# Moving routing work into the prologue of a fused attention and expert kernel, and reordering its first loads

## The chip, the cores and the metric

The kernel runs on one core of one Trainium2 chip. The metric is the device time of one execution in microseconds, the median of three runs. A core has five engines that run their own instruction streams: TensorE (PE, with its weight loads shown apart as PEld), VectorE (DVE), ScalarE (ACT), GpSimd (POOL) and SyncE (SP). They wait for one another through semaphores. SyncE, ScalarE and GpSimd also issue DMA transfers, which sixteen DMA engines carry out.

## The reference

Two stages, one after the other. The first is attention with a relative position bias over 8 batches of 8 heads, 576 positions and head size 64. The second sends each of the 4608 rows of its output to one of 8 experts, chosen by a hash of the token's id, and applies a two-layer network.

```python
scores = scale * np.matmul(q, k.transpose(0, 1, 3, 2))
scores = scores + bias_table[bucket].transpose(2, 0, 1)[None]   # bucket: by |i - j|
attn = softmax(scores)
x = np.matmul(attn, v)            # then (B*S, H*D) = (4608, 512)

expert_idx = token_ids * np.int64(2654435761) % np.int64(E)     # E = 8
for e in range(E):
    mask = expert_idx == e
    h = np.maximum(x[mask] @ w1[e], 0.0)                        # 512 -> 1024
    out[mask] = h @ w2[e]                                       # 1024 -> 512
```

The multiplier leaves 1 modulo 8, so the expert is the lowest three bits of the id, which the kernel takes with a bitwise and.

## The kernel before

**Attention.** The work is cut into 32 pairs of heads (8 batches of 4 pairs), run in order by `for n in range(NP + 1)`. For each pair q and k are loaded as float32 (`load`, buffers qf and kf, four deep), cast to float16 by VectorE (`cast_q`, `cast_k`), transposed on TensorE through a PSUM tile with the tag "aux" (two buffers) and copied to SBUF by VectorE (`transpose_q` gives qt, `transpose_k` gives kz). kz holds two heads with zeros between them; `z_init` writes the zeros once for each of its three buffers. `scores(n, g)` for g = 0 to 3 multiplies kz by qt into a PSUM tile with the tag "ps" (two buffers of three banks), and ScalarE takes the exponential into att. The bias comes in as a factor: `band` multiplies parts of att by ebd on VectorE, a table of exponentials of the bias differences; `low_bands` does the rest of a pair one pair later. For the last key tile there is a compact copy, ebs, made by `make_ebs` with two transfers; before it is there `band` takes two half-height products from ebd. `av_steps(n - 1)` runs one pair behind: it multiplies att by vt and vs (values with a column of ones), then VectorE takes the reciprocal of the sums (rcp) and writes the normalised rows to x_all. v is cast by ScalarE (`cast_v`), the last 64 rows of each batch's v (vsf to vs) by GpSimd (`cast_vs`).

**Order.** All five engines follow an order written out by hand (`manual_schedule`): each engine executes its instructions in the order in which the Python code emits them. So a line's place in the code is its place in the queue of its engine.

**The bias table.** In the prologue the 32-bucket table (tbl) is multiplied by a constant one-hot matrix (ohsb) on TensorE, ScalarE takes the exponential (ebsb), and a transfer writes it to memory (F_d, shown as t_f). `load_bias` then reads it back with a shifted window for each row into ebd: pair 0 from the queues of ScalarE and SyncE, pair 1 and pairs 2 and 3 from GpSimd's.

**Routing.** `route()` is a generator; each `yield` ends a step, and the loops advance it. Its steps are: te (lowest bits of the ids in raw, two instructions of VectorE); tef (cast to float16); tps, ef (transposed to tokens on partitions by TensorE, mask added by VectorE) and the memsets of keep on GpSimd; oh (one-hot by expert); rps, inc, rnk (two matmuls into a tile with the tag "ps", a scan over it and a subtraction on VectorE); then mx, mxl with flag, a product, rank, ovf, sel and ds2, one step each. ds2 is the slot of each token in its expert's list. From n = 14 GpSimd writes the 40 lists of tokens to memory (`name_slot`, shown as t_id), three for a pair, paced by copies that wait for rcp.

**The first expert's rows.** At n = 28 SyncE reads the lists back (xid) and at n = 29 stores x of batch 6; at n = 30 GpSimd gathers five tiles of 128 rows for expert 0 (`gather(0, B - 1)`, xg). Rows of the last batch are not in memory then, so they come from x_all by a one-hot product: `hot_slots()` is a generator whose first step is an iota on GpSimd (ramp) and a copy of the slots (slot), and whose five further steps each compare ramp with one column (hot). It is advanced at g = 0, 1 and 3 of n = 30 and n = 31. `first_rows` transposes gathered tiles (xr, xt) within n = 31; `first_slots` does the one-hot product (xin).

**Experts.** For each of the 8 experts: hps (first layer), h, ops (second layer), and an indirect store of the rows by GpSimd.

Of the kernel before, what the change touches and what calls it, by code (L numbers as in the profile page):

```python
# [13 lines left out]
I32 = mybir.dt.int32  # L14
# [17 lines left out]
def kernel(  # L32
# [11 lines left out]
    nc = tc.nc  # L44
# [8 lines left out]
    P = 128  # L53
# [139 lines left out]
    with tc.tile_pool(name="at", bufs=1) as at, tc.tile_pool(  # L193
# [50 lines left out]
            if what == "qkv":  # L244
                load_v(n)

        def load_v(n):
            b, m = pairs[n]
            for hh in range(2):
                nc.sync.dma_start(  # L250
                    out=vf[n % 4][:, hh, :, :],
                    in_=v[b, 2 * m + hh, :NB4].rearrange(
                        "(t p) d -> p t d", p=P
                    ),
                )
# [16 lines left out]
        def cast_q(n):  # L272
            qh[n] = at.tile([PB, 2 * NBLK, 2, D], F16, name="qh", bufs=3)
            nc.vector.tensor_copy(  # L274
                out=qh[n][:, :, :, :].transpose([0, 2, 1, 3]),
                in_=qf[n % 4][:, :, :, :].rearrange(
                    "p h k (c d) -> p h (k c) d", c=2
                ),
            )
# [238 lines left out]
        def band(n, g, lo=0):  # L518
            m = pairs[n][1]
            att = atts[n]  # L520
            if g < NDUO:
                w0 = D * g - (HALF - P)
                hi = UA if lo == 0 else HALF
                a0, a1 = max(-w0, lo), min(WB - w0, hi)
                if a0 >= a1:
                    return
                part = (att[:, 2 * g : 2 * g + 2, :QW] if lo == 0 else
                        att[:, 2 * g : 2 * g + 2, QW:])
                a = part.rearrange("p c (o u) -> p c o u", o=2)[
                    :, :, :, a0 - lo : a1 - lo  # L530
                ]
                nc.vector.tensor_tensor(  # L532
                    out=a, in0=a,
                    in1=ebd[:, :, m, :, a0 + w0 : a1 + w0].transpose(
                        [0, 2, 1, 3]
                    ),
                    op=ALU.mult,
                )
            else:
                a = att[:, NU - 1, :QW].rearrange("p (o u) -> p o u", o=2)[  # L540
                    :, :, :EW
                ]
                if n < NPAIR:
                    for hh in range(2):
                        w0 = EW - HD * hh
                        r = slice(D * hh, D * hh + D)
                        nc.vector.tensor_tensor(
                            out=a[r], in0=a[r],
                            in1=ebd[r, :, m, hh, w0 : w0 + EW], op=ALU.mult,
                        )  # L550
                else:
                    nc.vector.tensor_tensor(
                        out=a, in0=a, in1=ebs[:, :, m, :], op=ALU.mult
                    )
# [102 lines left out]
        )  # L657
        ohsb = at.tile([2 * NB, FW], F16, name="ohsb")
        nc.scalar.dma_start(out=ohsb[:, :], in_=OH_d.ap())
        nc.gpsimd.dma_start(out=ident[:, :], in_=I128_d.ap())  # L660
        load(0, "qk")
        load(1, "qk")

        def z_init(i):
            nc.vector.memset(kz[i][D:P, :S].bitcast(I32), 0)
            nc.vector.memset(kz[i][:D, S:].bitcast(I32), 0)

        idle = at.tile([P, 512], F16, name="idle")
        nc.vector.memset(idle[:, :].bitcast(I32), 0)
# [36 lines left out]
                )  # L706

        z_init(1)
        z_init(2)
        FH = FW // 2  # L710
        for i in range(2):
            nc.tensor.matmul(
# [9 lines left out]
        nc.scalar.dma_start(  # L722
            out=F_d.ap(), in_=ebsb[:, :, :].rearrange("h a b -> h (a b)")
        )
        def load_bias(eng, m0, m1, b2):
            for o in range(2):
                eng.dma_start(
                    out=ebd[b2::2, o, m0:m1, :, :].rearrange(
                        "p m h w -> p (m h) w"
                    ),  # L730
                    in_=bass.AP(
                        F_d.ap().tensor,
                        2 * m0 * FW + (o - b2 + 1) * FY + 1,
                        [[1, D], [FW, 2 * (m1 - m0)], [1, WB]],
                    ),
                )

        def make_ebs():
            for hh in range(2):
# [6 lines left out]
                    ),  # L746
                )

        cast_q(0)
        cast_k(0)  # L750
        v_init(0)
        vs_init(0)
        for i in range(1, 4):
            v_init(i)
        nobody = at.tile([P, NSLOT // P, 2], I32, name="nobody")
        nc.gpsimd.memset(nobody[:, :, :], BIG)
        load_bias(nc.scalar, 0, 1, 0)
        load_bias(nc.sync, 0, 1, 1)
        load(0, "v")
        load(2, "qk")  # L760
        load_vs(0, nc.gpsimd)
        ids = moe_token_ids.bitcast(I32).rearrange(
            "(b s c) -> b s c", b=B, c=2
        )
        nc.gpsimd.dma_start(out=raw[:1, :, :], in_=ids[B - 1 :])
        nc.gpsimd.dma_start(out=raw[1:, :, :], in_=ids[: B - 1])
        nc.gpsimd.dma_start(out=msk[:, :], in_=MSK_d.ap())
        nc.gpsimd.dma_start(out=cnt[:, :], in_=CNT_d.ap())
        transpose_q(0)
        keep_busy(idp[:, :], 1)  # L770
        transpose_k(0)
        keep_busy(idp[:, :], 1)
        cast_q(1)
        cast_k(1)
        routing = route()
        advance(routing, 2)
        nc.gpsimd.tensor_copy(out=pace[:, :], in_=kh[1][:1, 0, 0, 0:1])
        for b2 in range(2):
            load_bias(nc.gpsimd, 1, 2, b2)
# [25 lines left out]
        for n in range(NP + 1):  # L805
# [10 lines left out]
            b, m = pairs[n]  # L816
            if n == 1:
                vs_init(1)
            if n == 3:
                make_ebs()  # L820
            if b + 1 < B and m == 1:
                load_vs(b + 1)
# [12 lines left out]
                (load_w1 if w == 1 else load_w2)(e, y, y + w)  # L835
            for g in range(NSG + 1):
                scores(n, g)
                if 3 <= n < 14 and g == 1:
                    next(routing, None)
                if n == NP - 3 and g == 1:  # L840
                    store(B - 2, 0, NIT)
                if n == NP - 2 and g == 0:
                    gather(0, B - 1)
                if n == NP - 1:
                    for sc in ((), (1,), (2, 3), (4,))[g]:
                        first_rows(sc)
                if NP - 2 <= n and g in (0, 1, 3):
                    next(hotting, None)
                if n == 0:
                    if g == 1:  # L850
                        transpose_q(1)
                        transpose_k(1)
                        advance(routing, 2)
                        band(n, 0)
                    elif g == 2:
                        band(n, 1)
                        band(n, 2)
                    elif g == 3:
                        cast_v(0)
                        band(n, 3)  # L860
                        band(n, NDUO)
                        load(4)
                elif n == 1:
                    if g == 0:
                        low_bands(0)
                        cast_k(2)
                        cast_q(2)
                    elif g == 1:
                        advance(av, 27)
                        band(n, 0)  # L870
                    elif g == 2:
                        advance(av, 99)
                        band(n, 1)
                        band(n, 2)
                    elif g == 3:
                        transpose_k(2)
                        transpose_q(2)
                        cast_v(1)
                        load_v(5)
                        band(n, 3)  # L880
                        band(n, NDUO)
                        cast_k(3)
                        cast_q(3)
                elif g == 0:
                    if n < NP - 1:
                        transpose_k(n + 1)
                    low_bands(n - 1)
                    advance(av, 12)
                elif g == 1:
                    if n == 2:  # L890
                        transpose_q(3)
                        cast_v(2)
                        load_v(6)
                        cast_q(4)
                    if n + 2 < NP:
                        cast_k(n + 2)
                    if 2 < n < NP - 1:
                        cast_v(n + 1)
                    advance(av, 15)
                    band(n, 0)  # L900
                elif g == 2:
                    if n < NP - 3:
                        cast_q(n + 3)
                    if n == 2:
                        cast_v(3)
                    advance(av, 99)
                    band(n, 1)
                    band(n, 2)
                elif g == 3:
                    if n < NP - 2:  # L910
                        transpose_q(n + 2)
                    band(n, 3)
                    band(n, NDUO)
# [218 lines left out]
```

The softmax here doesn't subtract the row's maximum and nothing guards it: scores larger than these inputs give would overflow.

## Time and profile before

| | |
|---|---|
| time, median of three runs | 383.17 us (382.03 to 384.43) |
| profiled span | 377.3 us |
| PE busy | 329.2 us (87%) |
| ACT busy | 237.2 us (63%) |
| DVE busy | 218.7 us (58%) |
| POOL busy | 186.3 us (49%) |
| chain of waits: PE, DVE, DMA, ACT, POOL | 52%, 18%, 9%, 7%, 4% |
| mean DMA rate | 175 GB/s |

The span falls into three parts. The first scores start at 8.87 us; the attention loop runs from there to about 222 us; the expert stage runs from 222.29 us, its first matmul, to the end. In the row of slices the shares of VectorE and ScalarE are at 8 and 9 tenths in the loop and fall off behind it. A share of the whole span mixes the parts, so a wait in the loop is read from the engine's own timeline there. A timeline line gives the start and length in microseconds, the engine, line, operation and tiles, and in brackets how long the engine had been idle before it and what released it. For example, `[0.41 <-ACT att L507]` in the loop means that ScalarE had been idle for 0.41 us. A row of the windows view gives, for one stretch, the busy time of each engine, the granted clock of TensorE, the mean busy share of the DMA engines (which can be over 1 where packets overlap) and the rate.

### The profile page before, as it was taken

How to read it: one execution, taken by the hardware profiler on the slowest of the kernel's cores; microseconds unless marked ns; L12 is line 12 of the kernel's file. 1: busy time of each engine (PE TensorE's matmuls, PEld its weight loads, DVE VectorE, ACT ScalarE, POOL GpSimd, SP SyncE). 2: the span in 40 equal slices, each digit the busy share in tenths (PEclk: the TensorE clock that was granted, in tenths of full speed). 3: DMA queues.
4: the chain of work that ended last, by engine and by line, in shares of the span. 5: the costliest groups of instructions: out<-in, count | busy, mean ns of one | idle time of the engine just before them, and what ended most of it. 6: DMA issues, size and time to landing. Idle time of an engine off the chain costs nothing.

```text
span 377.3 us, 8871 instructions
## 1 busy us (share of the span) xinstructions
PE 329.2 (87%) x3463; PEld 220.1 (58%) x3463; DVE 218.7 (58%) x593; ACT 237.2 (63%) x261; POOL 186.3 (49%) x304
## 2 busy tenths in 40 slices
PE   7868888898888988989784779999999999999991
PEld 2545665666666766666562556566665656565650
DVE  5889999999999999999941740212121212112121
ACT  2857888989988989889955315454544444444420
POOL 7801010221258848758425007588679677742322
PEclk9989999999999999999969799999999999999997
DMA  7899997998978999998841014849999999997212
GB/s 173 200 254 245 228 207 183 211 208 205 219 152 181 197 246 166 179 232 150 175 67 55 3 64 91 214 101 200 241 199 246 236 257 227 215 204 136 89 59 83
DMA packets 125525, 66.01 MB, mean 175 GB/s; under 512 B 86326, under 2 KB 117695, under 8 KB 125474
## 3 DMA queue, kind: packets, MB, share of 16 engines
q0 software_dynamic: 19744, 31.90, 41.3%
q1 hardware_dynamic: 105346, 33.25, 37.5%
q8 instruction: 29, 0.48, 0.5%
q10 hardware_dynamic: 384, 0.21, 0.2%
q14 instruction: 22, 0.18, 0.2%
HBM read 68.28 MB, written 15.30 MB: 222 GB/s over the span
## 4 chain that ended last, share of the span: by engine, by line
PE 52%; DVE 18%; DMA 9%; issue 7%; ACT 7%; POOL 4%; SPq 2%; POOLq 0%; ACTq 0%; DVEq 0%
PE ops L977 18%; PE hps L953 18%; PE ps L502 7%; DVE att L532 6%; PE px L579 5%; ACT att L513 4%; DVE x_all L590 4%; DMA t_x<-x_all 3%; ACT vt L289 2%; PE xps L930 2%; DMA t_id<-pay,ds 2%; DMA kf<-in_k_dram 2%; DVE qh L274 1%; DMA vf<-in_v_dram 1%; DVE rcp L589 1%
## 5 line engine op out<-in xcount | busy, mean ns | idle before, releaser
L513 ACT ACTIVATE att<-ps 128x1536 f16<-128x1536 f32 x96 | 138.6, 1448 | 40.5 <-PE ps L502 25.7
L502 PE MATMUL ps<-qt,kz 128*128 128x512 f16 (+1 forms) x576 | 94.9, 294 | 23.9 <-ACT att L513 21.2
L984 DVE COPY ok<-ops 128x512 f32<-128x512 f32 x40 | 27.7, 692 | 120.5 <-PE ops L977 109.6
L579 PEld LDWEIGHTS <-att 128*128 128x128 f16 x1440 | 76.7, 99 | 29.6 <-issue 10.6
L579 PE MATMUL px<-vt,att 128*128 128x98 f16 x1280 | 83.9, 210 | 7.8 <-DVE x_all L590 4.8
L977 PE MATMUL ops<-w2t,h 128*128 128x512 f16 x320 | 74.9, 379 | 0.0
L959 ACT ACTIVATE h<-hps 128x640 f16<-128x640 f32 x64 | 44.9, 704 | 42.8 <-PE hps L953 35.1
L532 DVE TENSOR_TENSOR att<-att,ebd 128x384 f16<-128x384 f16 (+2 forms) x192 | 70.0, 393 | 0.9
L953 PEld LDWEIGHTS <-w1t 128*128 128x128 f16 x512 | 50.1, 98 | 21.8 <-issue 1.4
L953 PE MATMUL hps<-xpt,w1t 128*128 128x320 f16 x448 | 62.0, 299 | 0.0
L985 POOL DMA_INDIRECT out_dram<-ok,xid x40 | 39.5, 988 | 45.1 <-DVE ok L984 35.1
L502 PEld LDWEIGHTS <-kz 128*128 128x128 f16 x576 | 37.2, 99 | 41.4 <-issue 25.8
L153 POOL DMA_INDIRECT xg<-t_x,xid x40 | 41.2, 1029 | 19.3 <-DMA t_x<-x_all 9.3
L977 PEld LDWEIGHTS <-h 128*128 128x128 f16 x320 | 30.1, 98 | 29.9
L619 POOL DMA_INDIRECT t_id<-pay,ds x40 | 41.8, 1044 | 8.8 <-issue 6.7
L934 ACT ACTIVATE xpt<-xps 128x512 f16<-128x512 f16 x35 | 20.1, 596 | 37.1 <-PE xps L930 37.1
L579 PE MATMUL px<-vs,att 128*128 128x132 f16 x160 | 36.1, 226 | 2.3 <-POOL vs L267 1.8
L590 DVE TENSOR_TENSOR x_all<-px,rcp 128x384 f16<-128x384 f32 x64 | 31.4, 491 | 2.4 <-DVE rcp L589 0.2
L603 POOL COPY pace<-rcp 1x1 f32<-1x1 f32 x39 | 9.1, 233 | 42.9 <-DVE rcp L589 42.7
L267 POOL CAST vs<-vsf 64x256 f16<-64x256 f32 x16 | 7.5, 471 | 45.5 <-DMA vsf<-in_v_dram 27.7
L507 ACT ACTIVATE att<-ps 128x576 f16<-128x576 f32 x32 | 20.8, 651 | 1.1 <-PE ps L502 1.1
L289 ACT ACTIVATE vt<-vf 128x512 f16<-128x512 f32 x32 | 19.9, 623 | 0.1
(84 smaller groups left out, 266.5 us busy)
## 6 DMA issues: line engine op xcount, KB each, us to landing
qf<-in_q_dram SPq DMA_DIRECT2D x32, 288.0 KB
kf<-in_k_dram SPq DMA_DIRECT2D x32, 288.0 KB, 4.5
vf<-in_v_dram SPq DMA_DIRECT2D x64, 128.0 KB, 5.2
w1t<-in_moe_w_dram POOLq DMA_DIRECT2D x6, 1024.0 KB, 10.8
w2t<-in_moe_w_dram POOLq DMA_DIRECT2D x6, 1024.0 KB
t_x<-x_all SPq DMA_DIRECT2D x7, 512.0 KB
w1t<-in_moe_w_dram POOLq DMA_DIRECT2D x8, 256.0 KB
w2t<-in_moe_w_dram POOLq DMA_DIRECT2D x8, 256.0 KB, 7.2
```

What stands on the lines that cost most here:

```text
L153: nc.gpsimd.indirect_dma_start(out=xg[e % 3][:, sc, :], out_offset=None, in_=x_d.ap()[: S * nb, :], in_offset=bass.IndirectOffsetOnAxis(ap ...
L502: nc.tensor.matmul(out=out_ap, lhsT=z[:, k0 : k0 + P], rhs=rhs, start=True, stop=True,)
L513: nc.scalar.activation(out=att[:, 3 * g : 3 * g + 3, :QW], in_=ps[:, :, :], func=AF.Exp, bias=0.0, scale=scale,)
L532: nc.vector.tensor_tensor(out=a, in0=a, in1=ebd[:, :, m, :, a0 + w0 : a1 + w0].transpose([0, 2, 1, 3]), op=ALU.mult,)
L579: nc.tensor.matmul(out=px[:, ii, o : o + w], lhsT=lhsT, rhs=rhs, start=(y == 0), stop=(y == len(todo) - 1), skip_group_check=True,)
L590: nc.vector.tensor_tensor(out=x_all[:, b, its[0] : its[0] + ni, P * m : P * m + P].rearrange("p t (h d) -> p t h d", h=2), in0=pv[:, :, :, ...
L619: i = nc.gpsimd.indirect_dma_start(out=id_d.ap()[:, :], out_offset=bass.IndirectOffsetOnAxis(ap=ds2[:, g : g + 1], axis=0), in_=pay[:, g, ...
L953: nc.tensor.matmul(out=hps[:, nr, :NR], lhsT=w1h[:, kt, ts(ft, P)], rhs=xt[e][:, kt, ts(nr, NR)], start=(kt == 0), stop=(kt == NPT - 1),)
L959: nc.scalar.activation(out=h1[:, ft, :].rearrange("p (r n) -> p r n", r=NRC), in_=hps[:, :, :NR], func=AF.Relu, bias=0.0, scale=1.0,)
L977: nc.tensor.matmul(out=ops[:, :], lhsT=h1[:, ft, ts(kc, P)], rhs=w2h[:, ft, :], start=(ft == 0), stop=(ft == NFT - 1),)
L984: nc.vector.tensor_copy(out=ok[:, :], in_=ops[:, :])
L985: so = nc.gpsimd.indirect_dma_start(out=out[:, :], out_offset=bass.IndirectOffsetOnAxis(ap=xid[:, NSC * e + kc, 1:2], axis=0), in_=ok[:, : ...
```

## The change

Five things move; what is computed stays the same.

- The ids are read right after the constant one-hot matrix, from ScalarE's queue instead of GpSimd's; the mask and the count matrix are read early on GpSimd's queue.
- The first five steps of `route()`, up to inc and rnk, run in the prologue between the casts and transposes of pair 0. Before, two ran there, two in pair 0 and the fifth in pair 3. The sixth step, mx, comes at n = 5 instead of n = 4, and each later one pair later than before.
- SyncE loads q, k of pair 0 and q of pair 1, and then k of pair 1 and q, k of pair 2. A copy of one element from ebsb into kf[1] on ScalarE, emitted after the write of the bias table, makes these last loads wait until the write has been issued. In before, q and k of pair 2 came after the reads of the bias table and v of pair 0. The transposes of pairs 2 and 3 move earlier or later by one group accordingly.
- The zeros of the third kz buffer are written by GpSimd instead of VectorE, two filler matmuls (`keep_busy`) between the first transposes go, and ebs is made at n = 2 instead of n = 3.
- The first step of `hot_slots()`, with the iota, runs at n = 16; the five compares then run at the five places from n = 30, g = 0 to n = 31, g = 1, one place earlier each.

The diff, cut to its core:

```diff
+        nc.scalar.dma_start(out=raw[:1, :, :], in_=ids[B - 1 :])
+        nc.scalar.dma_start(out=raw[1:, :, :], in_=ids[: B - 1])
         nc.gpsimd.dma_start(out=ident[:, :], in_=I128_d.ap())
+        nc.gpsimd.dma_start(out=msk[:, :], in_=MSK_d.ap())
+        nc.gpsimd.dma_start(out=cnt[:, :], in_=CNT_d.ap())
         load(0, "qk")
-        load(1, "qk")
+        load(1, "q")
...
         z_init(1)
-        z_init(2)
...
         nc.scalar.dma_start(
             out=F_d.ap(), in_=ebsb[:, :, :].rearrange("h a b -> h (a b)")
         )
+        nc.scalar.activation(
+            out=kf[1][:1, 0, 0, 0:1], in_=ebsb[:1, 0, 0:1], func=AF.Copy,
+            bias=0.0, scale=1.0,
+        )
+        load(1, "k")
+        load(2, "qk")
...
+        routing = route()
+        advance(routing, 1)
         cast_q(0)
+        advance(routing, 1)
         cast_k(0)
+        load_bias(nc.scalar, 0, 1, 0)
+        load_bias(nc.sync, 0, 1, 1)
+        transpose_q(0)
+        advance(routing, 2)
         v_init(0)
         vs_init(0)
+        transpose_k(0)
+        advance(routing, 1)
+        load_vs(0, nc.gpsimd)
+        z_init(2, nc.gpsimd)
...
-        load_bias(nc.scalar, 0, 1, 0)
-        load_bias(nc.sync, 0, 1, 1)
-        load(0, "v")
-        load(2, "qk")
-        load_vs(0, nc.gpsimd)
...
-        transpose_q(0)
-        keep_busy(idp[:, :], 1)
-        transpose_k(0)
-        keep_busy(idp[:, :], 1)
+        load_v(0)
         cast_q(1)
         cast_k(1)
-        routing = route()
-        advance(routing, 2)
...
-            if n == 3:
+            if n == 2:
                 make_ebs()
...
-                if 3 <= n < 14 and g == 1:
+                if 5 <= n < 14 and g == 1:
                     next(routing, None)
...
-                if NP - 2 <= n and g in (0, 1, 3):
+                if n == 16 and g == 0 or NP - 2 <= n and g in (0, 1, 3):
                     next(hotting, None)
...
                     if g == 1:
                         transpose_q(1)
                         transpose_k(1)
-                        advance(routing, 2)
...
                     elif g == 2:
+                        transpose_k(2)
+                        transpose_q(2)
                         advance(av, 99)
...
-                        transpose_k(2)
-                        transpose_q(2)
...
                     if n == 2:
-                        transpose_q(3)
                         cast_v(2)
                         load_v(6)
+                        advance(av, 15)
+                        transpose_k(3)
                         cast_q(4)
...
                 elif g == 2:
+                    if n == 2:
+                        cast_v(3)
+                        advance(av, 99)
+                        transpose_q(3)
```

## The prediction

> **What bounds the kernel now.** I read the page's chain first (PE 52%, DVE 18%, DMA 9%, ACT 7%), then the chain in order of time, then each engine's timeline and waits where the diff touches them. The expert stage, 222.29 to 377 us, is TensorE's own (rows L953 and L977, 36% of the chain); the diff moves nothing in it. In the attention loop ScalarE sets the pace: a pair takes 5.75 us from exp to exp (99.43, 105.18, 110.93). So I look for stretches where ScalarE idles in that loop. There are three.
>
> *The start.* ScalarE's timeline, first exp of pair 2 and the next, then VectorE's with the cast before it (start, length, work, idle before it and releaser):
>
> ```profile
> 24.01 1.45 ACT L513 ACTIVATE att<-ps 128x1536 f16<-128x1536 f32 x1 [2.78 <-issue]
> 27.26 1.45 ACT L513 ACTIVATE att<-ps 128x1536 f16<-128x1536 f32 x1 [1.80 <-PE ps L502]
> ```
>
> ```profile
> 18.06 0.56 DVE L283 CAST kh<-kf 96x768 f16<-96x768 f32 x1 [1.36 <-DMA kf<-in_k_dram]
> ```
>
> The reader sees k of pair 2 arrive at 18.03, VectorE waiting, and pair 2's first exp 2.78 us late, its second 1.80 us more. From the DMA side (stretch, busy of PE, PEld, DVE, ACT, POOL, clock, DMA share, GB/s):
>
> ```profile
> 4.50:6.00 1.50, 1.50 (x4) 0.30 (x2) 0.90 (x3) 0.65 (x1) 1.44 (x5) 1.00 1.23 310
> 7.50:9.00 1.50, 1.27 (x9) 0.69 (x8) 0.66 (x3) 0.00 (x0) 1.32 (x3) 1.00 0.57 144
> 9.00:10.50 1.50, 1.50 (x4) 0.44 (x4) 1.47 (x4) 0.07 (x1) 0.07 (x1) 1.00 0.16 49
> 10.50:12.00 1.50, 1.50 (x16) 0.91 (x15) 1.13 (x4) 1.50 (x2) 1.50 (x3) 1.00 0.49 132
> ```
>
> 310 GB/s, then a hole with shares down to 0.16, while SyncE's queue holds the loads of pair 2 behind the bias table's round trip (its write: 5.18 to 8.91 in the chain).
>
> *The ranks in pair 3.* TensorE's timeline at the scores after the rank product:
>
> ```profile
> 36.17 0.81 PE L502 MATMUL ps<-qt,kz 128*128 128x512 f16 x3 [0.82 <-DVE rnk L348]
> ```
>
> rps takes one of the two ps buffers; scores wait until VectorE has read it (scan 0.83, subtraction 0.49).
>
> *The end.* The chain, then VectorE and ScalarE:
>
> ```profile
> 205.52 1.01 POOL xg L153
> 206.53 0.07 POOLq L404 x2
> ```
>
> ```profile
> 206.92 0.25 DVE L414 TENSOR_SCALAR hot<-ramp,slot 128x128 f16<-128x128 f16 x1 [7.67 <-POOL ramp L404]
> ```
>
> ```profile
> 212.32 1.45 ACT L513 ACTIVATE att<-ps 128x1536 f16<-128x1536 f32 x1 [7.55 <-PE ps L502]
> ```
>
> This is the largest wait of the loop. The iota for the first expert's slots stands on GpSimd behind five gathers, which wait for a store of x (idle 9.30); VectorE reaches the compare that reads it at 199.25 and stands still, with the normalisation TensorE needs queued behind it.
>
> **What the Trainium skill says.** "TensorE: Matmul & The Clock Gate", Part 1: GpSimd, VectorE and ScalarE take instructions in strict order. The 7.67 us agree: everything behind one compare stood still. The same part says that the clock halves after an idle window of about 3.4 us and needs a busy one to return; here the granted clock was 0.50 in 208 to 212, after the stall, and in 25.5 to 27, after the one at pair 2. "DMA: Bandwidth & Descriptors", Queues, rings and completion order: each issuing row has a ring per DMA engine, drained in turn with the others. That agrees with a 12 KB write taking 3.73 us beside 288 KB loads.
>
> **The change, part by part.**
>
> 1. *Ids first, routing in the prologue.* Two id transfers on ScalarE's queue cost 2 x 0.52 (row ohsb) ahead of its table load of 1.28: done at about 3.6, the exp of the bias is released at 4.33. Hidden. The ids, issued by 2.4, land between 4.2 (ohsb took 2.4) and 5.2 (ident took 3.3); I take 4.6. VectorE had two memsets at 4.38 to 5.07 and idled 0.51 before cast_q(0), 0.47 before cast_k(0), 0.81 before the kz copies. The memsets go to GpSimd; te (0.73) takes their place, tef (0.45) the second gap, ef and oh (0.23 + 0.49) the third. What stands in the open is inc and rnk, 0.83 + 0.49, after kz at 9.30. But te, tef, ef and oh leave the stretch 10.28 to 13.9, so the first bands still begin near 13.8. Scores (0,1) now wait for rnk, 10.65 for 10.2; at the slow clock (1.33 a set) the second exp moves by about 0.2, and if the gap keeps the clock down one window longer, by 0.8. I take 0.4 for ScalarE; the chain at pair 1 is VectorE's, so 0 there.
>
> 2. *k of pair 1, q and k of pair 2 behind the table's write.* A one-element copy on ScalarE (at most 0.2, idle there) holds SyncE until 5.95. Behind it stand only these loads and the bias reads. 3 x 288 KB at about 290 GB/s from 7.3 end near 10.5, inside the hole. cast_k(1) wants its k at 11.1: slack. k of pair 2 comes 7 us earlier. Casts of pair 2 then follow the low bands at 16.7: kh, qh to 17.7, then rcp, x_all, band(1,0) to 18.7. One new wait: GpSimd's bias loads of pair 1 follow cast_k(1), about 1.2 later, and land between 17.5 and 19.5 (the group took 4.4 each under load before); band(1,0) wants them at 18.4. I charge 0.7. The kz and qt copies end near 20.7 for 23.04 before; exp(2,0) starts at 22.4 for 24.01. The transposes of pair 3 come after the first part of av, so pair 2's second scores no longer wait for kh(3).
>
> From there VectorE sets the time: bands, casts and copies of pairs 1 and 2, in the new order, end pair 2's low bands at about 33.2 for 34.66. Gain 1.4.
>
> 3. *No ranks in pair 3.* 1.32 off VectorE where it is the chain, and the 0.82 wait on ps inside it: 1.3. ebs one pair earlier: one product of 0.25 for two of 0.25: 0.2. The later routing steps only move by one or two pairs.
>
> Sum of the start: 1.4 + 1.3 + 0.2, say 2.8. Does it reach the end? GpSimd from 102.0 on is back to back, and releases pair 28's vs at 189.55. It begins when rcp of the loop's fourteenth round releases it (idle 3.12), so it shifts with the loop, plus the iota now in between (0.07 + 0.26): net 2.5.
>
> 4. *iota and slot at n = 16, compares one slot earlier.* VectorE goes on at 199.3. By before's times, each step with its duration: x_all to 200.4 and 201.85, bands of pair 30 to 203.5, av of pair 30 on TensorE 203.2 to 206.1 around scores (31,1) at 204.3 (210.81 before: 6.5 gained). Then the gathers: issued 201.57, 202.90, 204.21, 205.52; landing takes at least 2.8 (row xg), so tiles 2, 3 and 4 land near 205.7, 207.0 and 208.3, later than the loop wants by up to 0.7. xr of tile 3 ends at 207.4, second av part 208.6, scores (31,3) 208.9, xr of tile 4 209.2, last bands of pair 31 near 211.0. From the last bands to hps it was 218.4 to 222.29, 3.9; so hps at about 214.9. All five compares are done, so the 0.83 wait of xin on hot goes, as does the slow clock of 205.8 to 212.7. Gain 7.4.
>
> Sum: 2.5 + 7.4 = 9.9. 383.2 - 9.9 = 373.3.
>
> **The rivals.** *A: the start gives nothing.* The ids land after 5.2, the clock stays down to 14.7, and pair 1's bias loads hold VectorE a full 1.5 with kz and qt of pair 2 behind. For it: DMA share is over 1.15 from 15 us on. Against: the hole is real and k of pair 2 has 6 us of slack. Then only part 4 stays: 383.2 - 7.4 = 375.8. *B: the gathers take the iota's place.* Landing 4 to 5 us, as gathers later do (median 7.8 in the row), holds TensorE in order at xr until about 211: gain 4 there, 383.2 - 4 - 2.5 = 376.7. Against: no other traffic stood in 200 to 208 (43 to 84 GB/s). *C: better.* The stall at pair 28's vs (1.84, and ScalarE's 2.79, 0.59, 0.45 behind it) shrinks because GpSimd starts with less lag, or the warm clock saves the 1.5 at pair 2: 371. *D: not faster.* It needs the prologue 4 us longer, from ids of over 7 us behind 288 KB loads, with B at the end on top: 383.2 + 4 - 4 = 383. Each id row is under 5 KB; I see little for it.
>
> **How the numbers follow.** Forecast 0.60, A 0.14, B 0.12, C 0.11, D 0.03. The range 369.5 to 377.5 holds the first four, with the spread of the three times before (382.03 to 384.43) at each side. Over 1% faster means below 379.4: all but D, 0.95; within 1% 0.04, slower 0.01.
>
> **What would show it.** Right: the DMA share of 9 to 10.5 over 0.8; no wait of kh on kf near 18; exp(2,0) by 22.5; no rps among the scores of pair 3; the hot compares without an idle before them, ramp near n = 16 on GpSimd; scores (31,1) about 2 us after (31,0); the expert stage as long as before. Wrong: te waiting for raw beyond 5.2, VectorE waiting for ebd at band(1,0) over 1.5, TensorE waiting long for xg at xr, or a new wait on GpSimd's iota in the middle of the naming of slots.

## The result, and the profile after

On the chip on which the prediction was made the changed kernel takes 372.91 us (median of four runs, 370.46 to 373.78) for 382.60 of the kernel before (381.38 to 384.43): a ratio of 0.9733, 95% interval 0.967 to 0.9795. (Ratios, the medians called undisturbed and the stages below leave out executions in a slower, disturbed state, into which the profiles of e5 and e9 fell, so a ratio can differ a little from the quotient of the other medians.) The forecast was 373.3, in a range of 369.5 to 377.5. The sum came out; three of the terms in it did not, and unaltered on two other chips the change gave much less. Both are told below.

**The end went as worked out.** First GpSimd's, then VectorE's timeline of the changed kernel:

```profile
116.29 0.25 POOL L404 IOTA ramp<- 128x128 f16 x1
```

```profile
199.50 0.25 DVE L414 TENSOR_SCALAR hot<-ramp,slot 128x128 f16<-128x128 f16 x1
199.98 0.20 DVE L589 RECIPROCAL rcp<-px 128x6 f32<-128x6 f32 x1 [0.23 <-PE px L579]
```

The iota is done 82 us before the first compare, which starts at 198.11; the second, shown here, is the one that stands where the first stood before, with 7.67 us of idle time then and none now, and the reciprocal behind it goes on at once. What stood in its way later, the transposes of the gathered rows on TensorE, and the first matmul of the expert stage:

```profile
205.21 0.40 PE L424 MATMUL xr<-ident,xg 128*128 128x128 f16 x4 [0.47 <-DMA xg<-t_x,xid]
206.79 0.40 PE L424 MATMUL xr<-ident,xg 128*128 128x128 f16 x4
208.15 0.40 PE L424 MATMUL xr<-ident,xg 128*128 128x128 f16 x4 [0.97 <-DMA xg<-t_x,xid]
...
215.12 1.11 PE L963 MATMUL hps<-xt,w1t 128*128 128x320 f16 x7 [0.38 <-DVE xt L448]
```

The gathers hold TensorE by 0.47 and 0.97, and hps comes at 215.12 for 222.29: 7.17 us earlier, where 9.9 were forecast, 7.4 of them from this step. From the first exponential of pair 30 to hps it takes 17.2 us for 25.4, 8.2 less; the loop came to pair 30 1.1 us later than before.

**The prologue came out later, not earlier.** In the kernel before, the cast to tef and the first exponentials:

```profile
11.11 0.45 DVE L308 CAST tef<-te 8x576 f16<-8x576 int32 x1
```

```profile
10.44 2.79 ACT L513 ACTIVATE att<-ps 128x1536 f16<-128x1536 f32 x2 [5.28 <-PE ps L502]
```

In the changed kernel, VectorE's timeline where the ids arrive, GpSimd's beside it, and ScalarE's first exponential:

```profile
6.12 0.87 DVE L299 TENSOR_SCALAR te<-raw 8x512 int32<-8x512 int32 x2 [1.39 <-DMA raw<-in_moe_token_ids_dram]
6.92 0.54 DVE L274 CAST qh<-qf 96x768 f16<-96x768 f32 x1
7.39 1.05 DVE L308 CAST tef<-te 8x576 f16<-8x576 int32 x1
8.37 0.53 DVE L283 CAST kh<-kf 96x768 f16<-96x768 f32 x1
```

```profile
6.58 1.16 POOL L673 MEMSET kz<- 64x288 int32 x1
```

```profile
12.15 1.45 ACT L513 ACTIVATE att<-ps 128x1536 f16<-128x1536 f32 x1 [5.97 <-DMA ebd<-t_f]
```

The ids are used at 6.12, not 4.6, and VectorE waits 1.39 us for them with the casts of pair 0 behind. The cast to tef takes 1.05 us where the kernel before needed 0.45, beside a memset of GpSimd that takes 1.16 where such a memset takes 0.38 just ahead of it. The first exponential starts at 12.15; in the kernel before it was 10.44. (The releaser that its line names is a transfer whose data it does not read; its scores, begun at 10.59 on TensorE for 8.87 before, end at 12.12.) TensorE also stays slow for longer: six transposes take 0.42 us at 11.38 in the kernel before and 0.68 at 13.69 in the changed one. The prediction had named that case, at 0.8 us, and charged half of it.

Not all of this belongs to the order of the code. e2 and e12 below have the same prologue, and there the cast to tef takes 0.44 us and only GpSimd's memset is long; first GpSimd's, then VectorE's line of e2:

```profile
6.61 2.00 POOL L673 MEMSET kz<- 64x288 int32 x1
```

```profile
7.42 0.44 DVE L308 CAST tef<-te 8x576 f16<-8x576 int32 x1
```

Their first exponentials come at 11.6 and 11.5. So about 0.6 of the 1.7 us changes from one trace to the next.

The hole in the DMA's use did close: 9.0 to 10.5 us has a share of 1.27 and 253 GB/s, for 0.16 and 49.

```profile
9.00:10.50 1.50, 1.37 (x12) 0.75 (x9) 1.39 (x4) 0.00 (x0) 1.03 (x5) 1.00 1.27 253
```

**The middle took back what pairs 3 to 8 gave.** Starts of the first exponential of a pair, read from ScalarE's timelines, in us:

| pair | 0 | 2 | 5 | 8 | 16 | 26 | 30 | first hps |
|---|---|---|---|---|---|---|---|---|
| before | 10.4 | 24.0 | 46.0 | 64.0 | 110.9 | 169.9 | 196.8 | 222.3 |
| after | 12.2 | 24.1 | 44.5 | 62.1 | 109.3 | 174.0 | 197.9 | 215.1 |

Late by 1.7 at pair 0, level at pair 2, ahead by 1.9 at pair 8, and behind by 1.1 at pair 30. What is lost after pair 25 stands on GpSimd and TensorE, the first two lines from the changed kernel, the last from the kernel before:

```profile
166.84 0.40 POOL L267 CAST vs<-vsf 64x256 f16<-64x256 f32 x1 [6.03 <-DMA kf<-in_k_dram]
```

```profile
167.29 0.27 PE L579 MATMUL px<-vs,att 128*128 128x132 f16 x1 [4.46 <-POOL vs L267]
```

```profile
189.59 0.27 PE L579 MATMUL px<-vs,att 128*128 128x132 f16 x1 [1.84 <-POOL vs L267]
```

The cast of the last rows of v is queued behind the naming of slots on GpSimd and, as far as the trace tells, is released only when the scatters under way have landed (it names t_id for three of the four such waits, 11.6 us, and a load for this one); TensorE needs its result in the next pair. The same wait was there before (17.5 us in all on GpSimd, for 17.6 after), but it struck TensorE for 1.84 at pair 29 then and for 4.46 at pair 25 now. The two profiled spans differ by 6.4 us (377.3 and 370.9), while the medians differ by 9.7. The remaining 3.3 lie with the kernel before: its profiled execution took 379.21 us, less than each of its four timed runs, and that of the changed kernel 372.78, close to its median. So the trace on which the prediction was worked out shows an unusually quick execution, and what the others lost is in no trace.

### The profile page after: what moved, and what is told of

The parts are those of the page before. It is cut to its first block, busy times and chain, and to the rows that moved or that the text cites. A ratio compares the mean times of both kernels' runs of the same rounds, so it can differ in the third digit from the quotient of the medians.

```text
span 370.9 us, 8870 instructions
## 1 busy us (share of the span) xinstructions
PE 325.2 (88%) x3461; PEld 217.4 (59%) x3461; DVE 218.6 (59%) x590; ACT 237.1 (64%) x262; POOL 188.8 (51%) x304
## 4 chain that ended last, share of the span: by engine, by line
PE 52%; DMA 14%; DVE 14%; ACT 7%; issue 6%; POOL 2%; SPq 2%; ACTq 0%; POOLq 0%; DVEq 0%
PE ops L987 19%; PE hps L963 18%; PE ps L502 6%; PE px L579 5%; DMA vf<-in_v_dram 5%; ACT att L513 5%; DVE att L532 4%; DMA t_x<-x_all 3%; ACT vt L289 3%; DVE x_all L590 3%; PE xps L940 2%; DMA t_id<-pay,ds 2%; DMA ebd<-t_f 1%; DVE qh L274 1%; PE pk L472 1%
## 5 line engine op out<-in xcount | busy, mean ns | idle before, releaser
L502 PE MATMUL ps<-qt,kz 128*128 128x512 f16 (+1 forms) x576 | 93.5, 290 | 21.9 <-ACT att L513 21.5
L579 PEld LDWEIGHTS <-att 128*128 128x128 f16 x1440 | 74.9, 98 | 27.1 <-issue 7.7
L579 PE MATMUL px<-vt,att 128*128 128x98 f16 x1280 | 81.5, 207 | 2.7 <-DVE qt L465 1.0
L502 PEld LDWEIGHTS <-kz 128*128 128x128 f16 x576 | 36.4, 98 | 39.1 <-issue 25.8
L507 ACT ACTIVATE att<-ps 128x576 f16<-128x576 f32 x32 | 20.9, 652 | 2.3 <-PE ps L502 2.3
```

The costliest lines, as they stand in the source:

```text
L502: nc.tensor.matmul(out=out_ap, lhsT=z[:, k0 : k0 + P], rhs=rhs, start=True, stop=True,)
L579: nc.tensor.matmul(out=px[:, ii, o : o + w], lhsT=lhsT, rhs=rhs, start=(y == 0), stop=(y == len(todo) - 1), skip_group_check=True,)
```

## The experiments

They ran in three groups of four, each on a chip of its own, and none on the first one. The kernel before takes 389.81, 386.73 and 386.21 us there, so ratios to the kernel before of the same group are compared. A profile is one execution.

### First group: the iota, and the cast of vs

**e1, the iota alone,** on the kernel before:

```diff
-                if NP - 2 <= n and g in (0, 1, 3):
+                if n == 16 and g == 0 or NP - 2 <= n and g in (0, 1, 3):
                     next(hotting, None)
```

> The kernel before with one part alone: the first step of hot_slots (iota and slot copy) at n = 16, and with it each compare one place earlier. Theory: the end of the loop gives nearly all that was measured, 7.2 us from the last scores to the first expert matmul (222.29 against 215.12), so 382.6 - 7.2 = 375.4 us, with no wait of the compare on the iota and the first hps near 215 in the trace. Rival: the start's shorter waits carry half, and the gathers take the iota's place when the start is late as before: gain 4, 378.6 us.

Measured: 387.10 us, ratio 0.9886 (0.983 to 0.9942). That is nearer to the rival's ratio, 0.9895, than to the theory's, 0.981: the iota alone is worth 1.1% here, where the first chip's traces gave 7.17 us, 1.9%. The rival's reason is not in the trace, though: TensorE waits for no gathered rows, and no compare is held up.

**e2, everything but the iota:** the changed kernel with that line as it was.

```diff
-                if n == 16 and g == 0 or NP - 2 <= n and g in (0, 1, 3):
+                if NP - 2 <= n and g in (0, 1, 3):
                     next(hotting, None)
```

> The changed kernel with only the iota put back (first step of hot_slots at n = 30). Theory: the start alone is worth 1.8 to 2.2 us at pair 10 (exp at 76.00 before, 74.33 after), and the rest of the 9.7 goes: 372.9 + 7.2 = 380.1 us, with the compare idle for over 7 us behind the iota again. Rival: the start carries half of the gain, 377.7 us.

Measured: 387.73 us, ratio 0.994 (0.9916 to 0.9964). The ratio agrees with the expected 0.9935: without the iota, the start alone is worth 0.6% on this chip, with an interval that leaves out zero. The wait that is put back is smaller than on the first chip. VectorE's timeline of e2:

```profile
206.10 0.36 DVE L532 TENSOR_TENSOR att<-att,ebd 128x128 f16<-128x128 f16 x2
210.22 0.25 DVE L414 TENSOR_SCALAR hot<-ramp,slot 128x128 f16<-128x128 f16 x1 [3.76 <-issue]
```

and GpSimd's:

```profile
203.23 1.05 POOL L153 DMA_INDIRECT xg<-t_x,xid  x1 [8.06 <-DMA t_x<-x_all]
...
209.93 0.25 POOL L404 IOTA ramp<- 128x128 f16 x1
```

The compare waits 3.76 us, not 7.67: VectorE itself gets there only at 206.46 (199.25 in the kernel before on the first chip), because the loop is late, while the iota ends at 210.18 (206.88 there). What the compare waits is the time between these two, so a slow loop hides part of the iota's cost.

**e3, the cast of vs a pair earlier,** otherwise the changed kernel:

```diff
-            if b + 1 < B and m == 3:
+            if b + 1 < B and m == 2:
                 cast_vs(b + 1)
```

> The changed kernel with cast_vs one pair earlier (m == 2 for m == 3), so that GpSimd's cast of vs has a pair more of slack before TensorE needs it. In the changed kernel TensorE waited 4.46 us for it at pair 25. Theory: GpSimd's back-to-back run of naming slots (100.4 to 191.4 us) sets when the lists are complete, and through them the read-back, the store of x and the gathers; the wait at vs goes, but the gathers then hold TensorE at the first rows instead, so the gain is under 2: 371 to 373 us, with TensorE waiting 3 to 5 us on xg. Rival: the wait at vs is the bound by itself, and its 6.3 us (exp to exp of 12.06 for 5.75) come off: 366.6 us.

Measured: 384.94 us, ratio 0.9868 (0.982 to 0.9915). As a ratio the expectation was 0.970 to 0.975 and the rival's 0.958; neither came. Without the changed kernel in this group no gain or loss can be told. TensorE no longer waits for vs in the trace, but GpSimd does, ahead of the casts:

```profile
POOL vs L267 <- issue: 8.6, 2, 4.7
POOL vs L267 <- DMA t_id<-pay,ds: 3.5, 1, 3.5
```

(waited-for, us in all, times, longest, for 100 to 200 us), and pair 25 still takes 10.1 us to the next. There TensorE's matmuls have gaps, and ScalarE waits 3.77 us, for nothing that this trace names. So the direct wait of TensorE for vs is not all of it.

**e4, the casts of vs on VectorE** (all but batch 0):

```diff
-                nc.gpsimd.tensor_copy(
+                (nc.gpsimd if b == 0 else nc.vector).tensor_copy(
                     out=vs[b % 2][D * hh : D * hh + D, :, c0 : c0 + D],
```

> The changed kernel with the casts of vs from the second batch on VectorE instead of GpSimd. There they wait for the load of v alone; on GpSimd the second cast of each batch waits until the slot lists written so far have landed (2.4 to 6.0 us each, 17.5 in all in the changed kernel from 105 us on). Theory: GpSimd's run gets 15 us shorter, the wait of TensorE on vs goes, and the gathers come early: about 6 us off, 366 to 368 us, less some 0.3 a batch for 14 more casts on VectorE. Rival: VectorE is so full in the loop (9 tenths in most slices) that the casts cost what they save: 371 to 374 us.

Measured: 380.12 us, ratio 0.9689 (0.9625 to 0.9752): the fastest of its group, clearly faster than e3. As a ratio the expectation was 0.957 to 0.962 and the rival's 0.970 to 0.978; it lies between. It is taken up again in the third group.

### Second group: the parts of the start

**e5, the changed kernel again,** as the base of this group.

> The changed kernel unaltered, beside the next three, as their common base. The first chip gave a ratio of 0.973 to the kernel before. If the gain is a matter of the chip's loop speed alone it stays at 0.972 to 0.975; if some of it hangs on the stall of GpSimd in the middle (6.3 us at pair 25 in the first profile), which falls differently on another chip, it lies between 0.965 and 0.985. The first exp of pair 0 stays near 12.2 us and the first hps between 215 and 222.

Measured: 382.65 us (22 runs) for 386.73 (75 runs), ratio 0.9912 (0.9887 to 0.9937). This is the greatest surprise of the study: on this chip the change is worth 0.9%, not 2.7%. The interval of the first chip (0.967 to 0.9795) doesn't reach it, nor did the expectation.

**e6, the routing back in its old places,** loads as changed:

```diff
-        advance(routing, 1)
         cast_q(0)
-        advance(routing, 1)
         cast_k(0)
...
         cast_k(1)
+        advance(routing, 2)
...
-                if 5 <= n < 14 and g == 1:
+                if 3 <= n < 14 and g == 1:
                     next(routing, None)
...
                         transpose_k(1)
+                        advance(routing, 2)
                         band(n, 0)
```

> The changed kernel with the routing steps back where they were (te and tef behind the casts of pair 1, the transposes of the ids in pair 0, the rank product in pair 3), the loads in the new order. Theory 1: the routing in the prologue delays the first exp by 1.5 to 2 us (te waits for the ids until 6.1 us, and the casts of pair 0 stand behind it) and gives 1.3 to 2 us back in pair 3: first exp near 10.5, rank product in pair 3 again, exp of pair 8 within 0.5 us of the changed kernel's, and the time within 0.3% of it. Theory 2 (the prediction's): prologue free at VectorE's end, 1.5 us won in pair 3, so this kernel is 1.1 to 1.5 us slower at pair 8. Rival: the loads cause the late prologue, first exp stays near 12.

Measured: 383.17 us, ratio 0.9911 (0.988 to 0.9943), that of e5. VectorE's timeline of e6:

```profile
7.54 0.87 DVE L283 CAST kh<-kf 96x768 f16<-96x768 f32 x1 [1.31 <-DMA kf<-in_k_dram]
```

The first exponential comes at 11.3: 0.9 earlier than the changed kernel's 12.2 on the first chip, and 0.9 later than the 10.4 of the kernel before. So with the routing gone from it the prologue is still late, and that goes with k of pair 0, which is cast at 7.54 instead of 6.60. How much the routing costs is less sure: to e2's first exponential, with the routing in the prologue, the difference is 0.3 us. The load of k now shares the time with those of the ids, mask and counts; that these delay it was not tested alone. From pair 2 to pair 5 this kernel takes 21.9 us, and e7, which has no rank product in pair 3, 20.7: 1.2 us less, for 1.3 predicted. Of the others without that step e3 and e8 take 20.6 and 20.4, but e2 21.6, so the size holds only roughly. What the prologue saves here, pair 3 spends.

**e7, the loads in their old order,** routing as changed:

```diff
-        load(1, "q")
+        load(1, "qk")
...
-        nc.scalar.activation(
-            out=kf[1][:1, 0, 0, 0:1], in_=ebsb[:1, 0, 0:1], func=AF.Copy,
-            bias=0.0, scale=1.0,
-        )
-        load(1, "k")
-        load(2, "qk")
...
         load_v(0)
+        load(2, "qk")
         cast_q(1)
```

> The changed kernel with the loads in their old order (k of pair 1 up front without the one-element copy on ScalarE, q and k of pair 2 behind v of pair 0), routing in the prologue. Theory 1: the new order's gain is the wait for k of pair 2, so here VectorE waits for kf near pair 2 again, the exp of pair 2 starts 1.4 to 2.8 us later than in the changed kernel (25.5 to 27), pair 8 1.4 to 2 us later, and the time is 0 to 2 us longer, as far as GpSimd's back-to-back stretch does not swallow it. Rival: the ids land even later, behind k of pair 1 (te after 7 us, first exp after 13), and the loss is 3 us or more. Other rival: with the prologue later anyway, the old order loses nothing.

Measured: 383.11 us, ratio 0.9917 (0.9885 to 0.9948), that of e5 again. VectorE's timeline of e7 at k of pair 2:

```profile
18.24 0.36 DVE L532 TENSOR_TENSOR att<-att,ebd 128x128 f16<-128x128 f16 x2
18.52 0.55 DVE L283 CAST kh<-kf 96x768 f16<-96x768 f32 x1
```

No wait for k, though it is loaded late: with the prologue 1.7 us later, VectorE comes to this cast at 18.52, and the transfer, which was waited for until 18.06 before, has landed. The cast starts at the same 18.52 in the changed kernel. Pair 2 starts at 24.0 in e7 and at 24.1 in the changed kernel: the new order of the loads, worth 1.4 us in the prediction, gains nothing that the trace or the time shows once the routing stands ahead of it.

**e8, the ids first of all** on ScalarE's queue:

```diff
+        nc.scalar.dma_start(out=raw[:1, :, :], in_=ids[B - 1 :])
+        nc.scalar.dma_start(out=raw[1:, :, :], in_=ids[: B - 1])
         nc.scalar.dma_start(out=ohsb[:, :], in_=OH_d.ap())
-        nc.scalar.dma_start(out=raw[:1, :, :], in_=ids[B - 1 :])
-        nc.scalar.dma_start(out=raw[1:, :, :], in_=ids[: B - 1])
```

> The changed kernel with the two id loads ahead of the one-hot table on ScalarE's queue. Theory 1: te waits for the ids because they are issued second and third, beside the q and k loads; here te starts at 4.8 to 5.5 us for 6.1, the first exp of pair 0 at 11 to 11.5 for 12.2, pair 8 0.5 to 1 us earlier, the time 0 to 1 us shorter. Rival A: the ids take that long whatever their place in the queue (few and long rows), te still near 6, nothing gained. Rival B: the one-hot table comes later by as much, the exp of the bias table, its write and the loads behind it move by 1 us, and the bands of pair 0 wait for ebd: 0.5 us slower.

Measured: 382.80 us, ratio 0.9919 (0.9887 to 0.9951), no gain. VectorE's timeline of e8:

```profile
4.07 0.95 DVE L299 TENSOR_SCALAR te<-raw 8x512 int32<-8x512 int32 x2
...
7.05 0.97 DVE L283 CAST kh<-kf 96x768 f16<-96x768 f32 x1 [0.77 <-DMA kf<-in_k_dram]
8.88 0.46 DVE L465 COPY qt<-pq 128x576 f16<-128x576 f16 x1 [0.85 <-PE pq L457]
9.41 0.23 DVE L316 TENSOR_TENSOR ef<-tps,msk 128x40 f32<-128x40 f16 x1
```

The ids are there at 4.07, two microseconds earlier, so their place in the queue did make them late. But k of pair 0 and the transposes take over the wait: ef comes at 9.41, for 9.25 in the changed kernel, and the first exponential at 12.0.

### Third group: does GpSimd absorb the gain?

**e9, the changed kernel,** base of this group.

> The changed kernel unaltered, common base of this group. It gave 0.973 of the kernel before on the first chip and 0.991 on another one. If the chip's own loop speed in the stretch from pair 16 to pair 30 decides, the ratio falls between these and goes with that stretch: 88.6 us there gave 0.973, 95.2 us gave 0.991.

Measured: 383.56 us for 386.21 (undisturbed 381.48 for 385.81), ratio 0.9872 (0.9802 to 0.9943). Again less than on the first chip, though its interval comes close to the one there (up to 0.9795).

**e10, the changed kernel with the casts of vs on VectorE** (the edit of e4).

> The changed kernel with the casts of vs of batches 1 to 7 on VectorE instead of GpSimd, so that no cast stands behind the naming of slots. Theory 1: GpSimd's second cast of vs in each batch waits 17.5 us in all for the scatters to land, and this back-to-back engine sets the stretch from pair 16 to 30 and swallows what the start gains; without it that stretch takes 86 to 89 us for about 95, and the time is 1.5 to 2.2% (6 to 8 us) below the changed kernel of this group. Rival: VectorE is full (18 to 19 of 20 us busy), the 14 casts of about 0.4 us cost it 5 to 6 us, and nothing is won.

Measured: 377.06 us, ratio 0.9748 (0.9699 to 0.9797): 4.4 us below e9 by the undisturbed medians, 1.3% by the ratios, a little under the expected 1.5%. Pairs 16 to 30 take 87.9 us, within the expected 86 to 89. What GpSimd waits for between 100 and 200 us, first in e7, which has the casts on GpSimd:

```profile
POOL vs L267 <- DMA t_id<-pay,ds: 17.7, 4, 5.3
POOL pace L603 <- DVE rcp L589: 5.2, 4, 3.1
```

then in e10:

```profile
POOL pace L603 <- DVE rcp L589: 11.3, 8, 5.0
```

In e10 no instruction of GpSimd waits there for landings of the scatters; GpSimd has caught up and waits for the loop instead. Against that stands a new wait on VectorE:

```profile
182.75 0.59 DVE L267 CAST vs<-vsf 64x256 f16<-64x256 f32 x2 [3.47 <-DMA vsf<-in_v_dram]
```

**e11, the kernel before with the same casts on VectorE.**

> The kernel before with the same casts on VectorE, nothing else changed. Theory 1: with GpSimd out of the way the change is worth its two parts in full, about 7 at the end and 1 to 2 at the start, so this kernel is 2.0 to 2.5% (8 to 9.5 us) slower than the changed one with the same casts, at a ratio of 0.985 to 0.995 to the kernel before. Rival: the stretch is as long for both and the casts help both alike; then this kernel is only 0.9% slower than its changed counterpart, at a ratio near 0.978.

Measured: 382.68 us, ratio 0.9933 (0.9905 to 0.9962), in the band that the first theory gave for it. With GpSimd's wait gone the change is worth 0.9748 / 0.9933 = 0.981, or 5.5 us by the undisturbed medians, less than the expected 8 to 9.5; with it, in the same group, 0.987 and 4.3 us. These lie so close, and their intervals overlap so far, that no difference is shown.

In the traces the lead goes through: in e10 pair 8 starts at 64.9 for 67.3 in e11, 2.4 earlier, and pair 30 at 200.8 for 203.0, still 2.2 earlier. On the first chip a lead of 1.9 at pair 8 was a lag of 1.1 at pair 30. But it goes through with the casts on GpSimd too: e2 has the new start and e1 the old one, on one chip, and e2 leads by 2.1 at pair 8 (62.7 and 64.8) and by 2.1 at pair 30 (204.8 and 206.9). So the casts on GpSimd do not swallow the lead as a rule. The compare of e11:

```profile
207.00 0.25 DVE L414 TENSOR_SCALAR hot<-ramp,slot 128x128 f16<-128x128 f16 x1 [1.28 <-issue]
```

It waits only 1.28 us, since the loop is later still against the gathers.

**e12, as e10 with eight buffers for the reciprocal:**

```diff
-                rcp = at.tile([P, 3, 2], F32, name="rcp", bufs=4)
+                rcp = at.tile([P, 3, 2], F32, name="rcp", bufs=8)
```

> As the second kernel of this group (casts of vs on VectorE), with eight buffers for the reciprocal instead of four. GpSimd's pace copies read the reciprocals, so a late GpSimd can hold VectorE at a reciprocal. Theory 1: once the casts are gone from GpSimd it keeps up (it waited 11.4 us for reciprocals), nothing is won by more buffers, within 0.3% of the second kernel. Rival: VectorE still waits for GpSimd there, and the time falls by another 1 to 4 us.

Measured: 379.92 us, ratio 0.9839 (0.9784 to 0.9894), 2.9 us slower than e10, which neither theory had. The intervals overlap slightly. Its profile has a longer wait for the load of vsf,

```profile
158.30 0.73 DVE L267 CAST vs<-vsf 64x256 f16<-64x256 f32 x2 [3.96 <-DMA vsf<-in_v_dram]
```

in one of the pairs; whether the buffers bring that about stays open. With the casts on VectorE no gain from more reciprocals is seen. With the casts on GpSimd, where GpSimd is later, e12 says nothing, but a trace does. VectorE's longest wait of e2 in the loop, and GpSimd's copy behind that reciprocal:

```profile
176.71 0.20 DVE L589 RECIPROCAL rcp<-px 128x6 f32<-128x6 f32 x1 [4.82 <-remote]
```

```profile
177.03 0.18 POOL L603 COPY pace<-rcp 1x1 f32<-1x1 f32 x1 [0.59 <-DVE rcp L589]
```

GpSimd had read the reciprocal four earlier, whose buffer this one takes, 9 us before, and waits for this one; the matmuls that it reads had ended 4.8 us before. So it isn't a late GpSimd that holds VectorE here. TensorE, ScalarE and VectorE go on at 176.58, 176.69 and 176.71, TensorE first, after a gap for which its timeline names no releaser.

### The stages side by side

From ScalarE's timelines and the first hps, in us:

| kernel | pair 0 | pair 8 | 16 to 26 | 26 to 30 | 30 to hps | wait of the first compare |
|---|---|---|---|---|---|---|
| before (first chip) | 10.4 | 64.0 | 59.0 | 26.9 | 25.4 | 7.67 |
| after (first chip) | 12.2 | 62.1 | 64.7 | 23.9 | 17.2 | none |
| e1 iota alone | 10.7 | 64.8 | 67.4 | 27.0 | 20.0 | none |
| e2 old iota | 11.6 | 62.7 | 69.3 | 25.5 | 20.9 | 3.76 |
| e3 cast earlier | 12.2 | 62.3 | 67.3 | 27.2 | 16.8 | none |
| e6 routing late | 11.3 | 63.2 | 69.3 | 24.8 | 19.7 | none |
| e7 loads early | 12.2 | 62.3 | 68.5 | 28.4 | 17.4 | none |
| e8 ids first | 12.0 | 62.4 | 70.2 | 26.5 | 19.1 | none |
| e4 casts on VectorE | 12.2 | 63.4 | 60.5 | 28.0 | 19.0 | none |
| e10 the same | 12.0 | 64.9 | 60.3 | 27.6 | 20.6 | none |
| e11 the same, before | 10.4 | 67.3 | 61.5 | 26.7 | 22.2 | 1.28 |
| e12 with 8 buffers | 11.5 | 64.4 | 64.2 | 26.9 | 18.8 | none |

Two columns carry the reading, each from one trace of a kernel. From pair 16 to 26, the stretch with most of the naming of slots and the loads of weights, the kernels with the casts on GpSimd take 67 to 70 us on the other chips, and those with the casts on VectorE 60 to 64. From pair 30 to hps, each kernel with the old iota and its nearest relative without it (before and after, e2 and e3 on one chip, e11 and e10 on one chip) differ by 8.2, 4.1 and 1.6 us, close to the wait of its compare, 7.67, 3.76 and 1.28. Only the first of these is beyond doubt: kernels without the wait range from 16.8 to 20.6 themselves, and against e1, on the same chip, e2 takes only 0.9 more. In this stretch VectorE waits at one reciprocal for 2.63 us in e1, 2.45 in e8 and 2.00 in e10, though the matmuls that it reads had ended over 2 us before, and not so in the changed kernel on the first chip.

## Why the prediction was right, and where it was not

*Part 4, the iota.* The mechanism held, and on the first chip the size: 8.2 us from pair 30 to hps for 7.4, with the gathers holding TensorE 0.97 at most (0.7 predicted). Rival B, the gathers in the iota's place, fell. What the prediction lacked was that this gain depends on a difference of two arrival times: the compare waits 3.76 and 1.28 us where the loop runs later, and e1, the iota alone, gives 1.1%.

*Part 1, ids and routing in the prologue.* The steps that failed were the landing at 4.6 and the 0.4 us for ScalarE. The ids were used at 6.12, the cast to tef took 1.05 for 0.45 (not in e2 and e12), k of pair 0 comes later as well (e6, e8), and the first exponential moved by 1.7. The prediction's own mark of a wrong forecast, te waiting for raw beyond 5.2, is in the trace. "The chain at pair 1 is VectorE's, so 0 there" fell with it: it is VectorE that is late.

*Part 2, the loads.* The hole filled as said and k of pair 2 was not waited for, but exp(2,0) came at 24.10, not 22.4. The term of 1.4 us is not seen: e7, without the new order, starts pair 2 just as early and takes the same time, as far as its interval of 0.3% either way tells. A wait was taken away where the work ahead of it had just become longer.

*Part 3, no ranks in pair 3.* From pair 2 to pair 5 before takes 22.0 us and after 20.4, 1.6 for the predicted 1.3 + 0.2; e6 against e7 gives 1.2 for the ranks alone, one trace of each.

*Does the start reach the end?* The prediction let 2.5 us through, as GpSimd "shifts with the loop". On the first chip's traces the lead was 1.9 at pair 8 and gone by pair 30, and there rival A, "the start gives nothing", describes the traces better than the forecast does. In the first group the start did reach the end: e2, the change without the iota, is 0.6% faster than the kernel before, 2.2 us by the undisturbed medians. Which of its edits bring that is not known. e6, e7 and e8 each rearrange the start with no effect on the time that can be measured.

*Luck.* In the traces, which the sum was worked out on, hps comes 7.17 us earlier for the forecast 9.9, and the span is 6.4 shorter. The number came out because the sum was taken off the median of timed runs, 383.17, which is 4.0 us above the execution in the trace, and the timed runs then differed by more than the traces. The iota is a right reading of the end; that the whole came to 373 is in part luck, as the ratios of 0.991 and 0.987 on two other chips say.

*Left open.* Why the stretch from 16 to 26 takes 59.0 us in the kernel before on the first chip and 67 in e1 on another is not settled; the trace before is of an unusually quick execution, and the kernel before was not profiled on the other chips. That the casts on GpSimd are part of it is shown by e4 and e10. How they lengthen the loop beyond the wait for vs is not: e3 takes that wait from TensorE and keeps the stall, and in e2 GpSimd has caught up where the loop stands longest. On the other chips TensorE has gaps in this stretch for which no releaser is named, 2.9 us in all in e1 to 6.6 in e2, and 1.1 to 4.1 with the casts on VectorE; the two traces of the first chip have none. Their cause stays open.

The fastest version of the third group is e10, 2.5% below the kernel before of that group, for 1.3% of the change alone.

## What to carry to other kernels

A small producer queued in order behind transfers that wait holds its reader for the difference of two arrival times; move it far ahead, and price it by both times and not by the idle time of one trace. A gain at the start may or may not reach the end: here the lead was gone by pair 30 in one pair of traces and whole in two others, so follow it pair by pair in the trace after, and measure that part alone. And where two edits touch one stretch, work out the second on the timeline that the first leaves: here the later prologue had already hidden the load that the second edit made earlier.

## What the runs showed of the hardware

- Small instructions of VectorE and GpSimd in the same stretch of the prologue took longer than elsewhere, and which of them did changed between executions of the same code. A cast of 8 rows on VectorE took 1.05 us for 0.45, beside a memset of 1.16 for 0.38, in the changed kernel and in e7. In e2 and e12 the cast took 0.44 and that memset 2.00. In e3 and e4 it was an instruction of te on VectorE (0.83 and 0.80 for 0.20) and a later memset of GpSimd (1.30 for 0.14). That the two engines hold each other is the nearest reading; it was not tested alone.
- A load of under 40 KB in few long rows, queued behind one other transfer while q and k are being loaded, was used 6.12 us into the span; issued first, it was there by 4.07 (e8). Unchanged, it was used between 5.94 (e10) and 6.32 (e4).
- The same kernel, the one before, takes 382.6, 386.2, 386.7 and 389.8 us on four chips. A gain of 2.7% on one of them was 0.9% and 1.3% on two others, so a change of this size wants more than one chip.
